# Output rows of two batches in nine 128-row blocks, and the folds of the modes in units 12 to 14

## The chip, the cores and the metric

The kernel runs on one core of one Trainium2 chip. The metric is the device time of one execution, in microseconds (us); the lower the better. Engines are named as in the profile: PE is TensorE's matmul, PEld its weight load, DVE is VectorE, ACT ScalarE, POOL GpSimd, SP SyncE.

## What is computed

A causal attention with decay over 8 batches, 8 heads, 576 positions and 64 elements a head, and then a layer that multiplies the lowest 64 Fourier modes of its input by complex 512 x 512 matrices:

```python
def _attn_ref(q, k, v, f):
    scores = scale * np.matmul(q, k.transpose(0, 1, 3, 2))
    cum = np.cumsum(np.log(np.clip(f, 0.0001, 1.0)), axis=-1)
    scores = np.where(causal, -1e9, scores + cum[:, :, :, None] - cum[:, :, None, :])
    ...
    return np.matmul(attn, v)

def _moe_ref(x, w_r, w_i, w_ch):            # x: 8 batches x 576 positions x 512
    X = np.fft.rfft(x, axis=1)              # 64 modes are kept: Xr, Xi
    Yr = np.einsum('bmd,mde->bme', Xr, w_r) - np.einsum('bmd,mde->bme', Xi, w_i)
    Yi = np.einsum('bmd,mde->bme', Xr, w_i) + np.einsum('bmd,mde->bme', Xi, w_r)
    ...
    y = np.fft.irfft(Y, n=S, axis=1)
    u = x + y
    return u + np.maximum(u @ w_ch, 0.0)
```

The two weight arrays are 64 MB each as given (64 x 512 x 512 x 4 bytes) and are read once. Inputs and output are f32; the kernel computes in bf16 with f32 sums.

## The kernel before

All instructions are issued in the order of the program text; no scheduler moves them. Each engine works through its own instructions in that order and waits on semaphores where it needs another's result.

**First stage: attention.** 32 pairs of heads, each with its loads, transposes, scores, exponentials and sums; x ends up in `x_all` (128 rows x 4 element blocks x 8 batches x 5 position blocks x 128). The 576 positions of a batch are five blocks: four of 128 and one of 64 (`SBLK`). Beside it run the Fourier sums of x (`XS`, `XP`) and the first weight tiles.

**The weights** are loaded by POOL, in tiles of 1 MB (`issue_w`, L140). Tile (u, dc) holds the four modes of unit u for the 128-row slice dc of both arrays (dc 0 and 1), or for a 256-row slice of one array (dc 2 and 3). The order is `wseq`: at the end (12, 1), (12, 2), (12, 3), (13, 1), ... (15, 3). The tiles lie in `wpool` (7 buffers); a load waits until the tile seven places ahead of it has been used. The very last tile, (15, 3), is loaded in four pieces of 256 KB, one for each mode.

**Second stage: the units** (loop at L717, u from 0 to 15). For each tile, `spec_mms` multiplies the Fourier columns by the weights, 8 matmuls on TensorE, into one PSUM tile `A`; at the end of a unit VectorE adds what the early tiles had given (`Yb`, L745), four matmuls turn it (`yps`, L748) and VectorE copies it to `YT` (modes of units 0 to 11) or `YL` (modes of units 12 to 15). The last unit is computed turned at once by `spec_cols` (L198, 32 matmuls a tile), its sum kept in `accT`. In units 2 to 10, `xw` computes x times w_ch for one batch each into `XW`. Batches 3 to 7 of `XW` lie in a buffer that the profile calls `yx`.

**The folds** (L670 to L714). From unit 12 on the modes of units 0 to 11 are complete, and the kernel adds their share of y to x and of y times w_ch to `XW`, in place, batch by batch: `fold_modes(b)` (8 matmuls, two copies on ScalarE) and `fold(b, ...)` (for each of five position blocks: two matmuls for `pu`, copied to `x_all` by ScalarE, and one for `pz`, added to `XW` by VectorE). Before the change two batches are folded in each of the units 12 to 15, at dc 1 and 2, ahead of the unit's matmuls for that tile; the last three position blocks of batch 7 come after `spec_cols` of tile (15, 2).

**Third stage: the output** (from L764). For a block of rows two PSUM tiles are made: U = x plus the modes of units 12 to 15, and Z = the same times w_ch. `bases` starts them with x and `XW` (a matmul by the identity, 128 or 64 rows in the contraction), `rest` adds the last 32 mode rows of the batch (contraction 32, from one of four 32-row groups of `BI4` and `yl`). Then ScalarE copies U to `u_sb` (L855), VectorE computes max(Z, 0) + U into `o_sb` (L856), and SP stores it (L861, L866). A block of before (`blocks`, `parts`) is one position block of two batches: two tiles of 128 rows, or, for the fifth position block, one tile in which each batch has 64 rows. There are 16 and 4 of these. `U`, `Z` and the sums of the last modes share two PSUM pools of four tiles each (`psU`, `psZ`).

`last_modes(h)` (L809) makes `yl[h]`, the last modes of four batches: 4 matmuls that turn `YL` (`pyl`), 8 that multiply it by w_ch (`pywl`), one copy on ScalarE and one on VectorE. It runs for h = 0 ahead of the first block, after the last tile of weights has been used (`AT2`, L837) and added into `YL` (L840), and for h = 1 ahead of block 7.

Of the kernel before, what the change touches and what calls it, by code (L numbers as in the profile page):

```python
# [10 lines left out]
F32 = mybir.dt.float32  # L11
BF16 = mybir.dt.bfloat16
I32 = mybir.dt.int32
ALU = mybir.AluOpType
# [3 lines left out]
def _strided(ap: bass.AP, free_dims, offset_elems: int = 0) -> bass.AP:  # L18
    new_ap = [list(ap.ap[0])] + [list(x) for x in free_dims]
    return bass.AP(tensor=ap.tensor, offset=ap.offset + offset_elems, ap=new_ap)  # L20
# [3 lines left out]
def kernel(  # L24
# [11 lines left out]
    nc = tc.nc  # L36
    B, H, S, Dh = q.shape
# [586 lines left out]
    with ExitStack() as bctx:  # L624
# [8 lines left out]
        with ExitStack() as mctx:  # L633
# [59 lines left out]
                nc.scalar.copy(yw_sb[:KF, :], pyw[:KF, :])  # L693
                return y_sb, yw_sb

            def fold(b, ys, sbs):

                y_sb, yw_sb = ys
                for sb in sbs:
                    Ms = SBLK[sb]  # L700
                    bi = BI[:KF, sb * 128 : sb * 128 + Ms]
                    pu = psX.tile([128, D], F32, tag="x", name="pu")
                    nc.tensor.matmul(
                        pu[:Ms, :], lhsT=ident_bf[:Ms, :Ms], rhs=x_all[:Ms, :, b, sb, :], start=True, stop=False
                    )
                    nc.tensor.matmul(pu[:Ms, :], lhsT=bi, rhs=y_sb[:KF, :], start=False, stop=True)  # L706
                    nc.scalar.copy(  # L707
                        x_all[:Ms, :, b, sb, :], pu[:Ms, :].rearrange("p (g c) -> p g c", g=NEB)
                    )
                    pz = psX.tile([128, D], F32, tag="x", name="pz")  # L710
                    nc.tensor.matmul(pz[:Ms, :], lhsT=bi, rhs=yw_sb[:KF, :], start=True, stop=True)
                    nc.vector.tensor_tensor(
                        XW[b][:Ms, sb, :], pz[:Ms, :], XW[b][:Ms, sb, :], ALU.add
                    )  # L714

            xw_plan = {2: 0, 3: 1, 5: 2, 6: 3, 7: 4, 8: 5, 9: 6, 10: 7}
            for u in range(NU):  # L717
# [4 lines left out]
                for dc in range(first, NEB - 1 if last else NEB):  # L722
                    if dc == NEB - 1 and u in xw_plan:
                        xw(xw_plan[u])
                    split = NSB
                    if u >= NF and dc < 3:
                        b = 2 * (u - NF) + dc - 1
                        split = 2 if b == B - 1 else NSB
                        ys = fold_modes(b)
                        fold(b, ys, range(split))  # L730
                    if last:
                        AT = psA.tile([128, NEB, 8, B], F32, tag="a", name="AT1")
                        spec_cols(AT, dc)
                        nc.vector.tensor_tensor(
                            accT[:], AT[:].rearrange("p e c b -> p e b c"), accT[:], ALU.add
                        )
                    else:
                        spec_mms(A, u, dc, dc == first, dc == NEB - 1)
                    issue_w()
                    if split < NSB:  # L740
                        fold(b, ys, range(split, NSB))
                if last:
                    break
                Yb = ybpool.tile([128, D], BF16, tag="yb", name="Yb")
# [19 lines left out]
        usb = bctx.enter_context(tc.tile_pool(name="usb", bufs=4))  # L764
        psU = bctx.enter_context(tc.tile_pool(name="psU", bufs=4, space=PSUM))
        psZ = bctx.enter_context(tc.tile_pool(name="psZ", bufs=4, space=PSUM))
        blocks = [(p, sb) for p in range(B // 2) for sb in range(NSB)]
        yl = {}

        def parts(n):  # L770

            p, sb = blocks[n]
            Ms = SBLK[sb]
            if sb < NSB - 1:
                return [(2 * p + k, k, slice(0, Ms), sb, Ms) for k in range(2)]
            return [(2 * p + k, 0, slice(Ms * k, Ms * k + Ms), sb, Ms) for k in range(2)]

        def bases(n):

            pts = parts(n)  # L780
            nt = 1 + pts[1][1]
            U = [psU.tile([128, D], F32, tag="u", name="U") for _ in range(nt)]
            Z = [psZ.tile([128, D], F32, tag="z", name="Z") for _ in range(nt)]
            for which, ps in enumerate((U, Z)):
                for b, k, rows, sb, Ms in pts:
                    nc.tensor.matmul(  # L786
                        ps[k][rows, :],
                        lhsT=ident_bf[:Ms, :Ms],
                        rhs=XW[b][:Ms, sb, :] if which else x_all[:Ms, :, b, sb, :],
                        start=True,  # L790
                        stop=False,
                    )
            return U, Z

        def rest(n, U, Z):

            for which, ps in enumerate((U, Z)):
                for b, k, rows, sb, Ms in parts(n):
                    r = (b + 2 * which) % 4
                    grp = slice(32 * r, 32 * r + 32)  # L800
                    nc.tensor.matmul(
                        ps[k][rows, :],
                        lhsT=BI4[grp, sb * 128 : sb * 128 + Ms],
                        rhs=yl[b // 4][which][grp, :],
                        start=False,
                        stop=True,
                    )

        def last_modes(h):  # L809

            py = psU.tile([128, D], F32, tag="u", name="pyl")
            for eb in range(NEB):
                nc.tensor.matmul(
                    py[:, eb * 128 : (eb + 1) * 128],
# [2 lines left out]
                    start=True,  # L817
                    stop=True,
                )
            pyw = psZ.tile([128, D], F32, tag="z", name="pywl")  # L820
            for eb in range(NEB):
                for n in range(2):
                    b = 4 * h + 2 * (1 - n)
# [4 lines left out]
                        start=(eb == 0),  # L828
                        stop=(eb == NEB - 1),
                    )  # L830
            yl[h] = [ylpool.tile([128, D], BF16, tag="yl", name="yl") for _ in range(2)]
            nc.scalar.copy(yl[h][0][:], py[:])
            nc.vector.tensor_copy(yl[h][1][:], pyw[:])

        first = bases(0)
        AT = psU.tile([128, NEB, 8, B], F32, tag="u", name="AT2")
        spec_cols(AT, NEB - 1)  # L837
        for h in range(2):
            bs = slice(4 * h, 4 * h + 4)
# [3 lines left out]
                accT[:, :, bs, :],  # L843
                ALU.add,
            )
        last_modes(0)
        for i, (p, sb) in enumerate(blocks):
            if i == 7:
                last_modes(1)
            U, Z = first if i == 0 else bases(i)  # L850
            rest(i, U, Z)
            o_sb = wpool.tile([128, 2, D], F32, tag="w8", name="o_sb")
            for n in range(len(U)):
                u_sb = usb.tile([128, D], F32, tag="usb", name="u_sb")
                nc.scalar.copy(u_sb[:], U[n][:])  # L855
                nc.vector.scalar_tensor_tensor(  # L856
                    o_sb[:, n, :], Z[n][:], 0.0, u_sb[:], ALU.max, ALU.add
                )
            s0 = sb * 128
            if len(U) == 2:  # L860
                nc.sync.dma_start(  # L861
                    out[2 * p : 2 * p + 2, s0 : s0 + 128, :].rearrange("b p e -> p b e"), o_sb[:]
                )
            else:
                for b, k, rows, _, Ms in parts(i):
                    nc.sync.dma_start(out[b, s0 : s0 + Ms, :], o_sb[rows, 0, :])  # L866


# [28 lines left out]
```

## Time and profile before

| | |
|---|---|
| time, median of 3 runs | 442.19 us (442.12 to 442.97) |
| the profiled execution: time | 442.61 us |
| the profiled execution: span of the core | 439.5 us |
| mean granted TensorE clock | 0.936 of full |
| PE busy | 346.6 us (79%) |
| DVE busy | 268.7 us (61%) |
| ACT busy | 233.3 us (53%) |
| DMA | 96.75 MB, mean 220 GB/s |

The span is the time from the first to the last instruction of the core; the time of a run has some 3 us around it. The busy shares are means over stages with different limits, so what a change in one stage does is read from that stage. All times of instructions below count from the start of the span. A matmul row such as "128*64 128x512" means 128 rows of contraction, 64 output rows (columns of the array) and a moving operand of 512 columns; the end of a matmul in the profile is modelled, so it is the distance from start to start that tells how long it holds the engine.

### The profile page before, as it was taken

The page shows a single profiled execution, that of the slowest core. Times are in us where ns is not written, and L with a number is a line of the kernel's source. Part 1 is how long each engine was busy: PE and PEld are TensorE (multiplying, and loading weights), DVE is VectorE, ACT ScalarE, POOL GpSimd, SP SyncE. Part 2 cuts the span into 40 slices and gives each one's busy share as a digit, 9 for nine tenths or more (in the row PEclk, how much of TensorE's full clock was granted, in tenths as well). Part 3 has the DMA queues.
Part 4 walks back from the last instruction along what each step waited for, and adds up shares of the span by engine and source line. Part 5 has one row for each costly group of instructions (what it writes and reads, how often), then busy time and mean ns, then how long its engine had stood idle before and what let it go on. Part 6 is the DMA issues. An engine that isn't in the chain of part 4 may idle for free.

```text
span 439.5 us, 10294 instructions
## 1 busy us (share of the span) xinstructions
PE 346.6 (79%) x4305; PEld 190.0 (43%) x4305; DVE 268.7 (61%) x641; ACT 233.3 (53%) x355; POOL 130.5 (30%) x201
## 2 busy tenths in 40 slices
PE   2678787888888989889793496697797688989993
PEld 1455555555555565555461232343333233334330
DVE  7588889777887778888871221223223255464884
ACT  6558767778777666566550022133222355454673
POOL 6544445434554444444213111112202221100000
PEclk9999999999999999999997589599979699799997
DMA  8999999999999999999999999999999999994698
GB/s 151 230 233 220 232 220 233 230 226 230 234 229 224 229 224 229 223 229 225 233 214 211 212 212 212 212 212 212 212 212 211 210 210 210 210 210 81 233 354 275
DMA packets 68221, 96.75 MB, mean 220 GB/s; under 512 B 3536, under 2 KB 45008, under 8 KB 68176
## 3 DMA queue, kind: packets, MB, share of 16 engines
q0 software_dynamic: 62960, 86.23, 105.5%
q1 hardware_dynamic: 5216, 9.88, 6.4%
q8 instruction: 33, 0.54, 0.4%
q14 instruction: 12, 0.10, 0.1%
HBM read 163.73 MB, written 9.44 MB: 394 GB/s over the span
## 4 chain that ended last, share of the span: by engine, by line
DMA 39%; PE 34%; DVE 19%; ACT 3%; issue 3%; POOL 1%; DVEq 0%; POOLq 0%; ACTq 0%
DMA w<-in_moe_w_i_dram 22%; DMA w<-in_moe_w_r_dram 15%; DVE vT L385 5%; DVE x_all L493 4%; DVE qkT L361 4%; PE pav L478 4%; PE A L194 4%; PE sps L433 3%; PE tv L383 3%; PE pd L522 3%; PE vp L394 2%; PE U L786 2%; PE Z L786 2%; DMA qk<-in_k_dram 2%; DVE vn L373 2%
## 5 line engine op out<-in xcount | busy, mean ns | idle before, releaser
L440 ACT ACTIVATE et<-sps 128x1024 bf16<-128x1024 f32 x96 | 96.0, 1050 | 12.5 <-PE sps L433 11.1
L478 PE MATMUL pav<-vs,et 128*128 128x65 bf16 (+1 forms) x896 | 51.3, 197 | 0.2 <-DVE vn L373 0.2
L745 DVE TENSOR_TENSOR Yb<-A,yx 128x512 bf16<-128x512 f32 x15 | 10.4, 692 | 65.2 <-PE A L194 65.2
L361 DVE COPY qkT<-tp 128x640 bf16<-128x640 bf16 x64 | 48.8, 763 | 1.4 <-PE tp L356 1.3
L478 PEld LDWEIGHTS <-et 128*128 128x128 bf16 (+1 forms) x896 | 36.5, 102 | 17.2 <-issue 13.3
L194 PE MATMUL A<-w,XP 128*16 128x512 bf16 (+1 forms) x240 | 23.0, 465 | 24.7 <-DMA w<-in_moe_w_i_dram 14.0
L661 PE MATMUL pxw<-wch,xT 128*128 128x512 bf16 (+1 forms) x160 | 40.9, 411 | 0.0
L433 PE MATMUL sps<-qkT 64*128 64x512 bf16 (+4 forms) x320 | 38.9, 306 | 1.1 <-DVE qkT L361 1.1
L493 DVE TENSOR_TENSOR x_all<-pav,rcp 128x384 bf16<-128x384 f32 (+2 forms) x96 | 36.2, 377 | 3.3
L356 PE MATMUL tp<-ident_bf,qk 128*64 128x128 bf16 x576 | 29.4, 232 | 8.6 <-DMA qk<-in_k_dram 8.6
L385 DVE COPY vT<-tv 128x576 bf16<-128x576 bf16 x32 | 24.2, 757 | 18.6 <-PE tv L383 18.6
L668 ACT CAST XW<-pxw 128x512 bf16<-128x512 f32 (+1 forms) x15 | 8.8, 585 | 47.7 <-PE pxw L661 47.7
L668 ACT CAST yx<-pxw 128x512 bf16<-128x512 f32 (+1 forms) x25 | 14.6, 585 | 34.5 <-PE pxw L661 34.5
L156 POOL DMA_DIRECT2D w<-in_moe_w_r_dram x27 | 20.5, 759 | 41.7 <-PE A L194 10.1
L165 POOL DMA_DIRECT2D w<-in_moe_w_r_dram x16 | 11.9, 741 | 69.8 <-PE A L194 44.7
L405 ACT COPY vs<-vp 128x576 bf16<-128x576 bf16 x32 | 20.5, 640 | 21.4 <-PE vp L401 21.4
L109 POOL DMA_DIRECT2D qk<-in_q_dram x32 | 19.6, 611 | 36.9 <-PE tp L356 9.0
L165 POOL DMA_DIRECT2D w<-in_moe_w_i_dram x19 | 13.2, 697 | 57.5 <-PE A L194 35.1
L707 ACT CAST x_all<-pu 128x512 bf16<-128x512 f32 (+1 forms) x40 | 23.4, 584 | 8.4 <-PE pu L706 7.5
L373 DVE TENSOR_TENSOR vn<-vt,wn 128x576 bf16<-128x576 f32 x32 | 23.8, 744 | 4.6 <-ACT wn L298 2.7
L492 DVE RECIPROCAL rcp<-pav 128x6 f32<-128x6 f32 (+2 forms) x96 | 16.2, 169 | 16.1 <-PE pav L478 16.0
L652 DVE COPY xT<-ptr 128x576 bf16<-128x576 bf16 x32 | 14.6, 458 | 18.1 <-PE ptr L647 17.4
(134 smaller groups left out, 669.3 us busy)
## 6 DMA issues: line engine op xcount, KB each, us to landing
w<-in_moe_w_r_dram POOLq DMA_DIRECT2D x16, 1024.0 KB, 29.7
w<-in_moe_w_i_dram POOLq DMA_DIRECT2D x15, 1024.0 KB, 31.6
w<-in_moe_w_r_dram POOLq DMA_DIRECT2D x27, 512.0 KB, 11.0
w<-in_moe_w_i_dram POOLq DMA_DIRECT2D x27, 512.0 KB, 12.6
vt<-in_v_dram POOLq DMA_DIRECT2D x31, 288.0 KB, 10.6
out_dram<-o_sb SPq DMA_DIRECT2D x16, 512.0 KB, 3.8
qk<-in_q_dram POOLq DMA_DIRECT2D x32, 144.0 KB, 10.7
qk<-in_k_dram POOLq DMA_DIRECT2D x32, 144.0 KB, 10.4
```

The source lines that it names most:

```text
L165: nc.gpsimd.dma_start(w8[:, j : j + step, :, :].rearrange("p m r e -> p m (r e)"), src[m : m + step, 256:512, :].rearrange("m (p r) e -> p ...
L194: nc.tensor.matmul(A[32 * j : 32 * j + M, :], lhsT=lhsT, rhs=rhs, start=st_, stop=sp_)
L356: nc.tensor.transpose(tp[64 * hp : 64 * hp + 64, r - r0, :, :].rearrange("p n c -> p (n c)"), qk[:, hp, r * 64 : r * 64 + 64], ident_bf[:, :],
L361: nc.vector.tensor_copy(st[i]["T"][:].rearrange("p n (c r) -> p n c r", r=9)[:, :, :, r0:r1], tp[:, 0 : r1 - r0, :, :].rearrange("p r n c ...
L373: nc.vector.tensor_tensor(vn[:], st[i]["vt"][:], _strided(wn[:, widx(i), :], [[1, 9], [0, Dh]]), ALU.mult)
L385: nc.vector.tensor_copy(st[i]["vT"][:].rearrange("p (c r) -> p c r", r=9), tv[:].rearrange("p r c -> p c r"))
L433: nc.tensor.matmul(ps[:, hp, c : c + n], lhsT=KT[sl, jb * 128 : jb * 128 + 128], rhs=QT[sl, i0 : i0 + n], start=True, stop=True,)
L440: nc.scalar.activation(st[i]["et"][:, T, :, :], ps[:], ACT.Exp, scale=scale)
L478: nc.tensor.matmul(pav[:Ms, sb % 3, hp, :], lhsT=eblk(i, hp, jb, sb), rhs=rhs, start=(jb == 0), stop=(jb == sb),)
L493: nc.vector.tensor_tensor(x_all[:ns, g, b, lo:hi, :].rearrange("p s (h d) -> p s h d", h=2), pav[:ns, lo % 3 : lo % 3 + n, :, 0:Dh], _stri ...
L661: nc.tensor.matmul(pxw[:Ms, :], lhsT=xT[:, eb, sb * 128 : sb * 128 + Ms], rhs=wch[:, eb, :], start=(eb == 0), stop=(eb == NEB - 1),)
L668: nc.scalar.copy(XW[b][:Ms, sb, :], pxw[:Ms, :])
```

## The change

- **Folds.** `fold` does all five position blocks at once, and three batches are folded in each of the units 12 and 13 (at dc 1, 2 and 3) and two in unit 14. None is left in unit 15.
- **Blocks of the output.** The 1152 rows of two neighbouring batches are taken together and cut in nine blocks of 128 (`cuts`): four in the first batch, one with 64 rows of each, four in the second batch, which start at position 64. The position blocks of `x_all` and `XW` are unchanged, so a block of the second batch has its bases from two matmuls of 64 rows: rows 64 to 127 of one position block go to output rows 0 to 63, rows 0 to 63 of the next to output rows 64 to 127. Its `rest` is one matmul for each of U and Z.
- **Steps.** There are 18 steps, two pairs of batches (P) times nine (n), each with two tiles: block n of the first two batches of P's four and block 8 - n of the other two. Every step has two full tiles, one ScalarE copy and one VectorE operation for each, and one store of 512 KB; the first and the last step store each tile by itself.
- **The first step.** All its bases for U and Z come ahead of the last tile of weights, as before. `last_modes` is taken apart: the copy of Z's modes is made in two halves on ScalarE and VectorE, U's `rest` comes ahead of it, and the sums for the other four batches (h = 1) are made in steps 0 and 1 instead of ahead of block 7.

```diff
                 nc.scalar.copy(yw_sb[:KF, :], pyw[:KF, :])
                 return y_sb, yw_sb
 
-            def fold(b, ys, sbs):
+            def fold(b, ys):
 
                 y_sb, yw_sb = ys
-                for sb in sbs:
+                for sb in range(NSB):
                     Ms = SBLK[sb]
                     bi = BI[:KF, sb * 128 : sb * 128 + Ms]
                     pu = psX.tile([128, D], F32, tag="x", name="pu")
@@ -722,12 +722,9 @@
                 for dc in range(first, NEB - 1 if last else NEB):
                     if dc == NEB - 1 and u in xw_plan:
                         xw(xw_plan[u])
-                    split = NSB
-                    if u >= NF and dc < 3:
-                        b = 2 * (u - NF) + dc - 1
-                        split = 2 if b == B - 1 else NSB
-                        ys = fold_modes(b)
-                        fold(b, ys, range(split))
+                    b = 3 * (u - NF) + dc - 1
+                    if 0 <= b < B:
+                        fold(b, fold_modes(b))
                     if last:
                         AT = psA.tile([128, NEB, 8, B], F32, tag="a", name="AT1")
                         spec_cols(AT, dc)
@@ -737,8 +734,6 @@
                     else:
                         spec_mms(A, u, dc, dc == first, dc == NEB - 1)
                     issue_w()
-                    if split < NSB:
-                        fold(b, ys, range(split, NSB))
                 if last:
                     break
                 Yb = ybpool.tile([128, D], BF16, tag="yb", name="Yb")
@@ -764,51 +759,53 @@
         usb = bctx.enter_context(tc.tile_pool(name="usb", bufs=4))
         psU = bctx.enter_context(tc.tile_pool(name="psU", bufs=4, space=PSUM))
         psZ = bctx.enter_context(tc.tile_pool(name="psZ", bufs=4, space=PSUM))
-        blocks = [(p, sb) for p in range(B // 2) for sb in range(NSB)]
+        rows_out = out.rearrange("b s e -> (b s) e")
+        steps = [(P, n) for P in range(2) for n in range(9)]
         yl = {}
 
-        def parts(n):
-
-            p, sb = blocks[n]
-            Ms = SBLK[sb]
-            if sb < NSB - 1:
-                return [(2 * p + k, k, slice(0, Ms), sb, Ms) for k in range(2)]
-            return [(2 * p + k, 0, slice(Ms * k, Ms * k + Ms), sb, Ms) for k in range(2)]
-
-        def bases(n):
-
-            pts = parts(n)
-            nt = 1 + pts[1][1]
-            U = [psU.tile([128, D], F32, tag="u", name="U") for _ in range(nt)]
-            Z = [psZ.tile([128, D], F32, tag="z", name="Z") for _ in range(nt)]
-            for which, ps in enumerate((U, Z)):
-                for b, k, rows, sb, Ms in pts:
+        def cuts(P, n, k):
+
+            n = 8 - n if k else n
+            b = 4 * P + 2 * k
+            if n < 4:
+                return [(b, 0, n, 0, 128)], [(b, 0, 128 * n, 128)]
+            if n == 4:
+                return [(b, 0, 4, 0, 64), (b + 1, 64, 0, 0, 64)], [(b, 0, 512, 64), (b + 1, 64, 0, 64)]
+            j = n - 5
+            return [(b + 1, 0, j, 64, 64), (b + 1, 64, j + 1, 0, 64)], [(b + 1, 0, 64 + 128 * j, 128)]
+
+        def bases(st_, ps, which):
+
+            for k in range(2):
+                for b, o, sc, lo, m in cuts(*st_, k)[0]:
                     nc.tensor.matmul(
-                        ps[k][rows, :],
-                        lhsT=ident_bf[:Ms, :Ms],
-                        rhs=XW[b][:Ms, sb, :] if which else x_all[:Ms, :, b, sb, :],
+                        ps[k][o : o + m, :],
+                        lhsT=ident_bf[lo : lo + m, lo : lo + m],
+                        rhs=XW[b][lo : lo + m, sc, :] if which else x_all[lo : lo + m, :, b, sc, :],
                         start=True,
                         stop=False,
                     )
-            return U, Z
-
-        def rest(n, U, Z):
-
-            for which, ps in enumerate((U, Z)):
-                for b, k, rows, sb, Ms in parts(n):
+
+        def rest(st_, ps, which):
+
+            for k in range(2):
+                for b, o, s0, m in cuts(*st_, k)[1]:
                     r = (b + 2 * which) % 4
                     grp = slice(32 * r, 32 * r + 32)
                     nc.tensor.matmul(
-                        ps[k][rows, :],
-                        lhsT=BI4[grp, sb * 128 : sb * 128 + Ms],
+                        ps[k][o : o + m, :],
+                        lhsT=BI4[grp, s0 : s0 + m],
                         rhs=yl[b // 4][which][grp, :],
                         start=False,
                         stop=True,
                     )
 
-        def last_modes(h):
-
-            py = psU.tile([128, D], F32, tag="u", name="pyl")
+        def two(pool, tag):
+            return [pool.tile([128, D], F32, tag=tag, name=tag.upper()) for _ in range(2)]
+
+        def modes_u(h, py):
+
+            yl[h] = [ylpool.tile([128, D], BF16, tag="yl", name="yl") for _ in range(2)]
             for eb in range(NEB):
                 nc.tensor.matmul(
                     py[:, eb * 128 : (eb + 1) * 128],
@@ -817,7 +814,9 @@
                     start=True,
                     stop=True,
                 )
-            pyw = psZ.tile([128, D], F32, tag="z", name="pywl")
+
+        def modes_z(h, pyw):
+
             for eb in range(NEB):
                 for n in range(2):
                     b = 4 * h + 2 * (1 - n)
@@ -828,12 +827,36 @@
                         start=(eb == 0),
                         stop=(eb == NEB - 1),
                     )
-            yl[h] = [ylpool.tile([128, D], BF16, tag="yl", name="yl") for _ in range(2)]
-            nc.scalar.copy(yl[h][0][:], py[:])
-            nc.vector.tensor_copy(yl[h][1][:], pyw[:])
-
-        first = bases(0)
+
+        def finish(U, Z, store):
+
+            o_sb = wpool.tile([128, 2, D], F32, tag="w8", name="o_sb")
+            for k in range(2):
+                u_sb = usb.tile([128, D], F32, tag="usb", name="u_sb")
+                nc.scalar.copy(u_sb[:], U[k][:])
+                nc.vector.scalar_tensor_tensor(
+                    o_sb[:, k, :], Z[k][:], 0.0, u_sb[:], ALU.max, ALU.add
+                )
+                store(o_sb, k)
+
+        def store_of(st_, single):
+
+            P, n = st_
+            R = [1152 * (2 * P) + 128 * n, 1152 * (2 * P + 1) + 128 * (8 - n)]
+
+            def store(o_sb, k):
+                if single:
+                    nc.sync.dma_start(rows_out[R[k] : R[k] + 128, :], o_sb[:, k, :])
+                elif k == 1:
+                    dst = rows_out[R[0] : R[0] + 128, :]
+                    nc.sync.dma_start(_strided(dst, [[(R[1] - R[0]) * D, 2], [1, D]]), o_sb[:])
+
+            return store
+
         AT = psU.tile([128, NEB, 8, B], F32, tag="u", name="AT2")
+        U, Z = two(psU, "u"), two(psZ, "z")
+        bases(steps[0], U, 0)
+        bases(steps[0], Z, 1)
         spec_cols(AT, NEB - 1)
         for h in range(2):
             bs = slice(4 * h, 4 * h + 4)
@@ -843,27 +866,30 @@
                 accT[:, :, bs, :],
                 ALU.add,
             )
-        last_modes(0)
-        for i, (p, sb) in enumerate(blocks):
-            if i == 7:
-                last_modes(1)
-            U, Z = first if i == 0 else bases(i)
-            rest(i, U, Z)
-            o_sb = wpool.tile([128, 2, D], F32, tag="w8", name="o_sb")
-            for n in range(len(U)):
-                u_sb = usb.tile([128, D], F32, tag="usb", name="u_sb")
-                nc.scalar.copy(u_sb[:], U[n][:])
-                nc.vector.scalar_tensor_tensor(
-                    o_sb[:, n, :], Z[n][:], 0.0, u_sb[:], ALU.max, ALU.add
-                )
-            s0 = sb * 128
-            if len(U) == 2:
-                nc.sync.dma_start(
-                    out[2 * p : 2 * p + 2, s0 : s0 + 128, :].rearrange("b p e -> p b e"), o_sb[:]
-                )
-            else:
-                for b, k, rows, _, Ms in parts(i):
-                    nc.sync.dma_start(out[b, s0 : s0 + Ms, :], o_sb[rows, 0, :])
+        py0 = psU.tile([128, D], F32, tag="u", name="pyl")
+        pyw0 = psZ.tile([128, D], F32, tag="z", name="pywl")
+        modes_u(0, py0)
+        nc.scalar.copy(yl[0][0][:], py0[:])
+        modes_z(0, pyw0)
+        rest(steps[0], U, 0)
+        nc.scalar.copy(yl[0][1][:, 0 : D // 2], pyw0[:, 0 : D // 2])
+        nc.vector.tensor_copy(yl[0][1][:, D // 2 : D], pyw0[:, D // 2 : D])
+        rest(steps[0], Z, 1)
+        pyw1 = psU.tile([128, D], F32, tag="u", name="pywl")
+        py1 = psZ.tile([128, D], F32, tag="z", name="pyl")
+        modes_u(1, py1)
+        finish(U, Z, store_of(steps[0], True))
+        nc.scalar.copy(yl[1][0][:], py1[:])
+        for i in range(1, len(steps)):
+            U, Z = two(psU, "u"), two(psZ, "z")
+            bases(steps[i], U, 0)
+            if i == 1:
+                modes_z(1, pyw1)
+                nc.vector.tensor_copy(yl[1][1][:], pyw1[:])
+            bases(steps[i], Z, 1)
+            rest(steps[i], U, 0)
+            rest(steps[i], Z, 1)
+            finish(U, Z, store_of(steps[i], i == len(steps) - 1))
 
 
 # ---- launch: one core; inputs and outputs as the reference has them ----
```

## The prediction

> **What bounds the kernel now.** I read the page's slices first (DMA at nine tenths for 36 of 40 slices, so almost all of the kernel is the stream of weights), then the DMA and PE views of the end of that stream, then the chain of waits behind it, because the diff touches only the time after 345 us.
>
> The end of the stream, in the timeline: the last issue on POOL, and TensorE's use of that tile (start, us).
>
> ```profile
> 383.74 0.53 POOL L165 DMA_DIRECT2D w<-in_moe_w_i_dram  x1 [4.92 <-DMA w<-in_moe_w_r_dram]
> ...
> 403.37 1.07 PE L211 MATMUL AT<-XP,w 128*128 128x16 bf16 x32
> ```
>
> The list of DMA issues, cut to that one (size, us to landing):
>
> ```profile
> w<-in_moe_w_i_dram POOLq DMA_DIRECT2D x1, 256.0 KB, 19.7
> ```
>
> Busy times by stretch (length; PE, PEld, DVE, ACT, POOL; clock, DMA share, GB/s):
>
> ```profile
> 403.00:404.00 1.00, 1.00 (x25) 0.76 (x25) 0.00 (x0) 0.00 (x0) 0.00 (x0) 1.00 0.03 8
> ```
>
> The last 256 KB of weights, issued at 383.74, land 19.7 later, at 403.44; the DMA rate is 8 GB/s in the microsecond around it, and 0 in the next. TensorE starts on this tile at 403.37. So two things end together there: the folds on TensorE and the stream. The chain of waits names TensorE only because it is the later by a hair.
>
> Behind that the chain is TensorE without a gap (start, us, what): one 64-row output block and one 128-row block.
>
> ```profile
> 424.99 0.33 PE U L786 x2
> 425.32 0.22 PE Z L786 x2
> 425.54 0.33 PE U L801 x2
> 425.87 0.01 PE Z L801 x2
> 425.88 0.54 PE U L786 x2
> 426.42 0.43 PE Z L786 x2
> 426.85 0.32 PE U L801 x2
> 427.17 0.01 PE Z L801 x2
> ```
>
> A 128-row block takes 1.30 (425.88 to 427.18), a 64-row block 0.89; 16 and 4 of them make 24.3 us; they and the second half's mode sums (L813 and L824, 1.3) fill 407.05 to 431.98. The first 512 KB store takes 2.8 from issue to landing; VectorE needs 0.65 for each output tile (nine in 5.88), so 1.31 per block, and ScalarE 1.07 for two: both just keep up.
>
> **The folds (units 12 to 14).** One fold is 5.13 on TensorE (359.86 to 364.99). After: unit 12 gets a third fold, so unit 13 starts at 359.86 + 5.13 = 364.99; its three folds and three weight tiles (0.55 each) and 0.93 for the way over Yb end at 382.96; unit 14 with two folds and three tiles at 395.8. All these tiles have landed by 388.4. Unit 15's first tile takes 0.9, to 396.7. Its second (issued 368.49, landing 30.0 later) comes at 398.5, the four chunks of its third between about 399.7 and 403.44. The later reads of tiles hold back issues on POOL: the tile of (15,1) is freed at 364 instead of 358.9, that of (15,3) at 376.4 instead of 371.2. The queue in front of them is 20 to 30 us deep (their times to landing), so the stream goes on and the landing at 403.44 stays; without that cover each us of lateness would cost one.
>
> What is gained: before, 32 matmuls followed 403.37 and the add to YL began at 404.48. After, 24 of them, at 0.028 each, are done as their chunks land; 8 remain, so YL starts at about 403.9: **-0.55**. The 15 us of work that leaves the stretch from 389.9 to 403.4 buys no more, since the stream ends it.
>
> **What the gap does to the clock.** TensorE now waits in most of 396.7 to 403.44 (0.9 for one tile, 1.2 for the first bases, 0.7 for three chunks). The trace shows what such a wait does. Windows of the clock's own grid (length, PE busy, granted clock, DMA share, GB/s):
>
> ```profile
> 304.50:307.91 3.41, 1.99 (x17) 1.00 1.12 210
> 338.63:342.05 3.42, 0.54 (x8) 0.99 1.18 207
> 342.05:345.46 3.41, 1.46 (x12) 0.50 1.19 208
> 345.46:348.87 3.41, 3.09 (x11) 0.51 1.15 212
> ...
> 369.35:372.77 3.42, 1.98 (x14) 0.99 1.19 208
> 372.77:376.18 3.41, 2.49 (x18) 0.50 1.19 211
> ```
>
> After a window with 1.98 or less of work the clock is halved for at least two windows; it comes back when these are filled. On this grid the next boundaries are 396.66, 400.07, 403.49, 406.90. The window to 400.07 would hold 0.9 + 0.6 of work, so the clock halves at 400.07 and returns at 406.90. In between lie, on the path: 8 matmuls (0.23 more at half clock), the transposing sum (0.43 for 0.24 in the folds at 345.78 and 390.02, so +0.25), and the second sum (0.98, all but its end at half clock: +0.9): **+1.4**. Bounds: the grid may lie otherwise. A boundary at 398.4 costs 0.8, one at 401.5 lets the clock fall only at about 404.9 and stay low to 411.7, which costs up to 3; none at all if TensorE comes to that gap late.
>
> **The head of the output.** The copy of the second sum (0.70 at 406.31, the bases of Z waiting for it) is cut in two halves on two engines: no such half is in the trace; between 0.35 (half) and 0.70, I take 0.42, nearest to half: **-0.3**. The 8+4 sums of the second half (1.3) move from block 7 to steps 0 and 1, where they partly cover the waits for buffers that step 0 holds: the U bases of step 1 wait for ScalarE's second copy, about 0.35. At full clock, with the gaps of before: YL 403.9, transposing sum 404.28, second sum 404.6, its copies 405.75, Z's modes 406.2, second half's first sum to 406.85, U bases to 407.5, second sum to 408.5, Z bases, and step 1's modes start at 409.15. Before, block 1's started at 408.35 with the 1.3 of sums still ahead.
>
> **The 18 steps.** Each step has one block of 128 rows in one batch (F) and, in its mirror, two pieces of 64 (a pair P), for U and for Z, then the modes R of K=32: F P F P R, or P F P F R. The 64-row blocks of before stood alone. What it costs to go from one shape to another, the timeline shows (start, us, matmul), in a fold's last block:
>
> ```profile
> 393.97 0.38 PE L711 MATMUL pz<-yw_sb,BI 96*128 96x512 bf16 x1
> 394.27 0.40 PE L703 MATMUL pu<-x_all,ident_bf 64*64 64x512 bf16 x1
> 394.60 0.40 PE L706 MATMUL pu<-y_sb,BI 96*64 96x512 bf16 x1
> 394.84 0.38 PE L711 MATMUL pz<-yw_sb,BI 96*64 96x512 bf16 x1
> 395.15 0.96 PE L211 MATMUL AT<-XS,w 128*128 128x16 bf16 x32
> ```
>
> From start to start: 0.30 from 128 columns to 64*64, 0.33 from there to 96*64, 0.24 within that shape, 0.31 out of it. Matmuls of one shape follow at 0.216 (393.75 to 393.97). So a change of shape adds 0.09 to 0.115, and a pair runs as one (two 64*64 in 0.24 at 418.75). A 128-row block has two changes, into and out of R: 5 x 0.216 + 0.22 = 1.30, as measured. A new step has five: 0.317 (R to F) + 0.307 + 0.330 + 0.307 + 0.306 = 1.567, or 0.315 + 0.330 + 0.307 + 0.330 + 0.312 = 1.594 in the other order. The step with n = 4 has pairs alone, but twice the modes, of which U's and Z's share row groups and go one after the other: 0.315 + 3 x 0.237 + 0.306 + 0.22 = 1.55. All 18: 8 x 1.567 + 8 x 1.594 + 2 x 1.55 = 28.4 against 24.3: **+4.1**. It is wholly on the path: VectorE (1.31), ScalarE (1.07) and a 512 KB store (385 GB/s at best in this stretch, 1.36) are all shorter. Bounds: 0 if the changes were hidden, +4.1; more only with the fourth rival.
>
> The Trainium skill, TensorEngine Tiling (Array Packing), section Key Properties, says that a change of tiling mode, unlike a change of tile, drains the array. It speaks against this mixing and gives no price; the rows above agree, at 0.09 to 0.115 each.
>
> **The end and the sum.** From the start of step 1's modes (409.15 at full clock) the other 16 steps, 25.25, lead to 434.4. The last modes to the end of the second tile: 2.33 (430.77 to 433.10 before). Its 256 KB store: before, a 512 KB one took 2.8 from issue to landing with queues empty and 128 KB took 4.2 behind a backlog; the slower steps leave none, I take 2.6. Landing to the end of the span: 1.2 (438.3 to 439.5). Full clock: 434.4 + 2.33 + 2.6 + 1.2 = 440.5; with the clock's 1.4: **441.9, against 439.5: +2.4**. In other words the last modes come 2.75 later at full clock (434.4 for 431.65), 1.7 of which the end gives back (6.1 for 7.85), since before a backlog of stores stood there (DMA full from 424 to 437), and the clock costs 1.4. The profiled execution took 442.61, 3.1 over its span and 0.42 over the median 442.19; +2.4 on the median is **444.6**.
>
> **Rivals.**
> 1. *The shape changes cost nothing here* (the pieces' weights are loaded ahead): steps of VectorE's 1.31 instead of 1.58, and soon DMA's 1.36. Modes of step 1 at 410.55, 16 x 1.33, then 2.33, 2.8 and 1.2: 438.2 or less; about 441, **faster**. It decides below some 1.42 per step. For it: two pieces in different quadrants could load early. Against: all five changes have a row, and none is free. 0.14.
> 2. *The clock stays up*, because TensorE reaches the gap late or the grid favours it: 440.5 span, 443.2. Against: every window under 1.98 in the rows dropped. 0.12.
> 3. *The clock falls late*, at a boundary after 404, and stays low into the steps: up to 1.6 more, 445.5 to 446.3. The Trainium skill, TensorE: Matmul & The Clock Gate, says that the window runs freely and does not restart with a kernel; no run here shows that. 0.20.
> 4. *The pair runs one after the other*: its two pieces come from different row halves and write one PSUM bank. 2 x 0.216 in 18 steps: +7.8, 452. The same skill's TensorEngine Tiling (Array Packing), Gotcha 1, says that row tiles may not use one bank at once. Against: the 32*64 modes of a 64-row block do just that and take 0.33, as those in separate banks do. 0.05.
>
> **How the numbers follow.** Forecast 0.49, rivals as given. The range 442.7 to 446.6 holds forecast, 2 and 3 (0.81); rival 1 lies below, rival 4 above. About 0.2% (0.9 us) is what a measurement can tell. Faster by more is most of rival 1: 0.13; within is its edge and that of rival 2: 0.06; slower 0.81.
>
> **What would show it.** PE's starts within a step: five gaps of 0.30 to 0.33 and steps near 1.58; no VectorE wait as the releaser. The last weights landing at 403.4 with TensorE waiting for them; a clock of 0.5 within 398 to 411. Steps of 1.3, or weights landing later than 404.5, would make the prediction wrong.

## The result, and the profile after

The changed kernel takes 447.53 us in the median of 5 runs (445.67 to 449.2) against 442.19 (441.04 to 443.06): a ratio of 1.0111, with an interval of 1.0071 to 1.015. By the ratio it is slower by 4.9 us, where +2.4 had been forecast: the side was right, the size too small by half, and 447.53 lies above the forecast's range (to 446.6).

The profiled execution has a span of 445.6 us (time 447.53, so 1.9 outside the span; the page before had 3.1 there, and the two spans differ by more than the times). Its chain of waits, from the last weights to the second step (start, us, what):

```profile
384.34 19.72 DMA w<-in_moe_w_i_dram
404.06 0.04 issue
404.10 0.42 PE AT L211 x8
404.52 0.02 issue
404.55 0.30 DVE YL L863
...
408.33 0.61 PE Z L795 x2
...
410.46 1.85 PE pywl L823 x8
412.31 1.10 PE Z L781 x3
413.42 0.53 PE U L795 x2
413.94 0.00 PE Z L795 x2
413.95 0.66 PE U L781 x3
414.60 0.66 PE Z L781 x3
415.26 0.32 PE U L795 x2
```

The chain before, at the same places:

```profile
404.48 0.30 DVE YL L840
...
406.31 0.70 DVE yl L833
407.01 0.04 issue
407.05 0.39 PE Z L801 x2
...
415.24 0.98 PE pywl L824 x8
```

After the change the chain starts with a transfer: TensorE waits for the last 256 KB, and only 8 matmuls and 0.49 us lie between the landing and the add to YL, where there were 1.04 (403.44 to 404.48). So the folds are out of the way, as the change says. But the 8 matmuls of the second half's sum take 1.85 at L823, where they took 0.98, and the modes of step 1 start only at 413.42. Behind that a step takes 1.64 (413.95 to 415.58), and the end follows 6.0 after the last modes, at 445.6.

The windows of the clock's grid show why the head is slow (length, PE busy, granted clock, DMA share, GB/s):

```profile
396.76:400.17 3.41, 1.62 (x54) 1.00 0.73 138
400.17:403.58 3.41, 2.89 (x31) 0.50 0.29 53
403.58:407.00 3.42, 2.68 (x26) 0.50 0.00 1
407.00:410.41 3.41, 2.97 (x15) 0.50 0.01 2
410.41:413.82 3.41, 3.41 (x17) 0.50 0.44 156
413.82:417.24 3.42, 3.42 (x26) 1.00 0.13 49
```

The clock falls behind the window with 1.62 of work, at 400.17, and is low for four windows, 13.65 us, until behind the first that is full. Before, the clock was 1.00 from 379.6 to 434.2.

### The profile page after: what moved, and what is told of

Read it like the earlier page. It is cut to its first block, busy times and chain, and to the rows that moved or that the text cites. A ratio compares the mean times of both kernels' runs of the same rounds, so it can differ in the third digit from the quotient of the medians.

```text
span 445.6 us, 10352 instructions
## 1 busy us (share of the span) xinstructions
PE 353.4 (79%) x4337; PEld 190.9 (43%) x4337; DVE 268.2 (60%) x641; ACT 233.8 (52%) x356; POOL 130.7 (29%) x201
## 4 chain that ended last, share of the span: by engine, by line
DMA 43%; PE 31%; DVE 18%; issue 3%; ACT 3%; POOL 1%; DVEq 0%; POOLq 0%; ACTq 0%
DMA w<-in_moe_w_i_dram 26%; DMA w<-in_moe_w_r_dram 15%; DVE vT L385 5%; DVE x_all L493 4%; DVE qkT L361 4%; PE pav L478 4%; PE A L194 3%; PE sps L433 3%; PE tv L383 3%; PE pd L522 3%; PE U L781 3%; PE Z L781 3%; PE vp L394 2%; DMA qk<-in_k_dram 2%; DVE vn L373 2%
## 5 line engine op out<-in xcount | busy, mean ns | idle before, releaser
L156 POOL DMA_DIRECT2D w<-in_moe_w_r_dram x27 | 20.5, 758 | 45.1 <-PE A L194 13.3
L405 ACT COPY vs<-vp 128x576 bf16<-128x576 bf16 x32 | 20.5, 640 | 21.4 <-PE vp L401 21.4
L837 DVE SCALAR_TENSOR_TENSOR o_sb<-Z,u_sb 128x512 f32<-128x512 f32 x36 | 23.2, 686 | 7.7 <-ACT u_sb L836 7.6
```

## The experiments

Every ratio is to the kernel before on the same chip. A difference of two ratios is given in us of 442. The changed kernel was not timed again beside the experiments, so a difference to it carries the intervals of both.

### e1_folds_back: the new output with the old folds

```diff
-                    b = 3 * (u - NF) + dc - 1
-                    if 0 <= b < B:
-                        fold(b, fold_modes(b))
+                    if u >= NF and dc < 3:
+                        b = 2 * (u - NF) + dc - 1
+                        ...
```

> The changed output (18 mixed steps, new first step), but the folds where they were before, in units 12 to 15. Theory (two costs: the empty stretch behind the folds halves TensorE's clock from 400.1 to 413.8, and a mixed step takes 1.64 instead of 1.30): TensorE has folds until 402, so the clock stays at 1.00 until the steps are done, the first weights-free work starts 0.5 later than in the changed kernel, the modes of step 1 start at about 409.8 instead of 413.36, steps stay at 1.64, span about 442, some 3.6 under the changed kernel and 2.5 over the kernel before. Rival A (the steps alone make the loss): no change, 445 to 446. Rival B (the clock alone makes it): span 439 to 440.

Measured: 1.0035 (1.0009 to 1.0062), 3.4 us under the changed kernel. In the profile the clock is 1.00 from 380.6 to 438.6, the steps take 1.64 and the span is 443.4 (some 442 expected); the add to YL, which starts the head, is at 405.24, and step 1's modes start 5.6 behind it, at 410.84 (409.8 expected). The forecast of 3.6 for the time holds; both rivals fall, since neither the steps alone (no change) nor the clock alone (equal to before) fits.

### e2_folds_only: the old output with the folds moved

```diff
-                        b = 2 * (u - NF) + dc - 1
+                    b = 3 * (u - NF) + dc - 1
+                    if 0 <= b < B:
+                        fold(b, fold_modes(b), range(NSB))
```

> The kernel before with nothing changed but the folds, moved to units 12 to 14. Theory: the clock falls at about 400 and is low through the head of the output and perhaps the first blocks; the last tile's sum is 0.5 earlier, the sums behind it and two or three blocks take twice their time: 2.5 to 3.5 over the kernel before, blocks at 1.30 behind that. Rival A (steps alone): 0 to 0.5 faster than before. Rival B (clock alone): 5 over before.

Measured: 1.0030 (1.0012 to 1.0047), 1.3 us slower than before: the same sign, less than forecast. The clock falls here too, at 401.5, but is back after 10.2 us, because the old head goes over to dense blocks sooner. Stores that stood in a queue at the end before may have room for a part of the delay, but the two profiles show little of that: from the landing of the last weights TensorE's last modes end 2.5 us later than before (30.3 for 27.8), as expected, and the span ends 2.2 later (38.3 for 36.1). Why the time shows 1.3 stays open; its interval reaches to 2.1. Blocks take 1.30 as ever. Both rivals fall: A said 0 to 0.5 faster, B 5 slower.

### e3_fill: work in the gap that nobody needs

```diff
+    def spin(ps, n):
+        for _ in range(n):
+            nc.tensor.matmul(ps[:], lhsT=ident_bf[:, :], rhs=wch[:, 0, :], start=True, stop=True)
...
+                        spin(psX.tile([128, D], F32, tag="x", name="pf"), 7 if dc == 1 else 2)
...
-        spec_cols(AT, NEB - 1)
+        spec_cols(AT, NEB - 1, lambda j: spin(pyw0, (0, 1, 4, 0)[j]))
```

> The changed kernel with 14 matmuls of 128x512 added whose results nobody reads: 7 behind the sum of tile (15,1), 2 behind (15,2), 1 and 4 behind the second and third piece of (15,3), all in time in which TensorE waits for weights. Theory: the windows of the clock's grid between 396.7 and 403.5 are filled, the clock stays at 1.00, and in spite of 3 us more work the span falls by 3 to 4 us, to about 442; the steps stay at 1.64. Rival (the wait for weights or the new head itself holds step 1 back, not the clock): no change or up to 0.5 slower.

Measured: 1.0013 (0.9994 to 1.0033), 4.3 us under the changed kernel, by adding 14 matmuls. The chain of this kernel over the same stretch as above:

```profile
405.70 0.38 ACT yl L882
406.08 0.02 issue
406.10 0.44 DVE yl L883
406.54 0.04 issue
406.58 0.39 PE Z L802 x2
406.97 0.33 PE pyl L817 x4
407.30 0.55 PE U L788 x3
407.85 0.98 PE pywl L830 x8
408.84 0.66 PE Z L788 x3
409.49 0.32 PE U L802 x2
```

The second sum is back to 0.98, and step 1's modes start 5.6 after the add to YL (403.87) instead of 8.9. The clock is 1.00 from 349.7 to 438.5. This is the clock's price in the changed kernel, shown: 4.3 us in the time, 3.3 of them in the head of these two profiles. The steps are still 1.64 (409.82 to 411.46).

### e4_two_changes_fewer: the same matmuls in another order

```diff
+        def both(st_, U, Z):
+            for k in range(2):
+                for ps, which in ((U, 0), (Z, 1)):
+                    for b, o, sc, lo, m in cuts(*st_, k)[0]:
...
-            bases(steps[i], U, 0)
             if i == 1:
...
-            bases(steps[i], Z, 1)
...
+            else:
+                both(steps[i], U, Z)
```

> The changed kernel with the bases of steps 2 to 17 in another order: both U and Z of the first tile, then both of the second, so that the shape of the matmul changes three times in a step instead of five. Same matmuls, same count. Theory (a change of shape costs 0.09 to 0.115): 1.64 becomes about 1.41 to 1.43, 16 steps save 3.4 to 3.7 us of the span; VectorE (1.31 a step) and the stores (1.36) are still shorter. Rival (the step is paced by VectorE, ScalarE or the buffers): unchanged, 1.64.

Measured: 1.0047 (1.0026 to 1.0068), 2.8 us under the changed kernel. A step in its chain of waits:

```profile
426.13 0.32 PE U L793
426.45 0.22 PE Z L793
426.66 0.33 PE U L793 x2
427.00 0.22 PE Z L793 x2
427.21 0.32 PE U L807 x2
427.53 0.01 PE Z L807 x2
```

1.41 a step (426.13 to 427.54) with the very matmuls that took 1.64: the second of two equal shapes takes 0.22, a change of shape 0.32 or 0.33. That is 0.11 for each of the two changes left out. The time gains less than 16 times 0.22 and less than the 3.4 to 3.7 expected: the stores (1.36 for 512 KB) then have little slack. DMA's share is over 0.93 in all but one of the 2 us stretches from 420 to 442, and from the last modes (437.23) to the end of the span (444.7) it is 7.5, where the changed kernel has 6.0.

### e5_fill_head: three matmuls in the head's short waits

The clock's fall had been forecast, its stay had not. This kernel leaves the gap as it is and fills only what TensorE waits behind it.

```diff
+        spec_cols(AT, NEB - 1, lambda j: spin(pyw0, (0, 0, 1, 1)[j]))
...
         rest(steps[0], U, 0)
+        spin(py0, 1)
```

> The changed kernel with three matmuls of 128x512 added whose results nobody reads, only in short waits of the head behind the fall of the clock: one between the last two pieces of the weights, one in the wait for YL, one in the wait for the copies of yl. The empty stretch before it stays, so the clock falls at about 400 as in the changed kernel. Theory (the clock comes back only behind a window of its grid that is filled; the head's own short waits of 0.35 to 0.45 keep two windows from it): the window from 403.6 is full, the clock is back after 6.8 us instead of 13.65, the span falls by 2.5 to 3.5 us. Rival (it comes back after a fixed time, or by something else than the fill): low for 13.65 as before, span unchanged or 0.5 longer.

Measured: 1.0083 (1.0052 to 1.0114), 1.2 us under the changed kernel in the time, though the intervals overlap; the mechanism shows in the profile:

```profile
396.76:400.17 3.41, 2.51 (x43) 0.98 0.61 115
400.17:403.58 3.41, 2.38 (x39) 0.50 0.15 26
403.58:407.00 3.42, 3.42 (x14) 0.52 0.01 2
407.00:410.41 3.41, 3.41 (x27) 1.00 0.42 149
```

The window from 403.58 is full now, and the clock is back behind it: 6.8 us low instead of 13.65. The weights landed 1.9 earlier against the grid in this execution, so the window holds another part of the head than in the changed kernel; without the added matmul of 0.54 it would have held some 2.9 (an estimate from its rows). From the add to YL (402.71) to the end of the span (441.5) it is 38.8 us, where the changed kernel has 41.1: 2.3 less, just under the 2.5 to 3.5 that were expected, and the time gains only half of that. A fixed time is ruled out: the clock is low for 6.8 here, 10.2 in e2 and 13.65 in the changed kernel.

### e6_fill_and_order, e7_folds_back_and_order: both costs away

These put the edits of e3 and e4 (e6) and of e1 and e4 (e7) together, with nothing added.

> e3_fill and e4_two_changes_fewer together: clock kept at 1.00 through the gap, three changes of shape in a step. Theory: step 1.42, so TensorE would be 3.5 us earlier than in e3_fill; but from there the stores (1.36 us per 512 KB at 376 KB per us) pace the end, and of 3.5 some 2.5 arrive: span about 439, 0.5 to 1.5 under the kernel before at the same landing of the weights. Rival (the shape changes and the clock are one and the same loss, or the end has another bound): no more than 1 us better than e3_fill.

> e1_folds_back and e4_two_changes_fewer together: folds where they were before, 18 steps with three changes of shape each. Theory: e1_folds_back less 16 times 0.22 on TensorE, less what the stores' backlog takes back: 2.5 to 3 us under e1_folds_back, between 0.5 faster than the kernel before and 1 slower. Rival: within 1 us of e1_folds_back.

Measured: 0.9992 (0.9973 to 1.0011) and 1.0013 (0.9994 to 1.0032). In e6 the clock is 1.00 from 349.4 to 434.7; in the profile of e7 it was 0.50 from 389.7 to 393.1, among the folds, and the add to YL came 2.4 behind the landing of the last weights, where it comes 1.4 behind it in e1. With the clock kept from there on and three changes of shape instead of five, the new output is as fast as the old, not faster; e6 gains 0.9 us on e3, e7 1.0 on e1, which is what the rival of each allowed, and under the 2.5 that the theory asked; against the kernel before, e7 lies where the theory had it, e6 just short of it. The stores take more of it than I reckoned: in e6 TensorE is done with its steps at 433, and DMA is full to 437. That they pace the end is read from this one profile; no run takes them away.

### e8_folds_and_fill: the folds' move by itself

```diff
+                        spin(psX.tile([128, D], F32, tag="x", name="pf"), 7 if dc == 1 else 2)
...
+        spec_cols(AT, NEB - 1, lambda j: spin(pyw0, (0, 1, 4, 0)[j]))
...
-        last_modes(0)
+        last_modes(0, pyw0)
```

That is e2 with the gap filled; the output is that of before.

> The output of before, the folds in units 12 to 14 (e2_folds_only), and the gap filled with the 14 matmuls nobody reads. Theory (moving the folds gains only that 24 of the last tile's 32 matmuls are done when its last piece lands, if the clock is kept): clock 1.00, 0.3 to 0.7 us faster than the kernel before. Rival A (the folds' move gains nothing even so): same as before. Rival B (it frees more than that, 15 us of work being out of the way): 2 or more faster.

Measured: 0.9969 (0.9951 to 0.9988), 1.4 us **faster** than before (0.5 to 2.2), the clock 1.00 from 348.3 to 433.7. So the move is worth something once the clock does not pay for it; the interval holds the upper part of the theory's 0.3 to 0.7, leaves out rival A, and B's 2 us stands at its edge. The profiles speak for the theory: from the landing of the last weights to the end of the span it is 35.5 us (402.8 to 438.3), where before it is 36.1, that is 0.5 less.

### e9, e10, e11: where the second half's sums stand

In e8 the new head was missing. e9 is e3 with the old blocks in its steps, and so has it:

```diff
-        steps = [(P, n) for P in range(2) for n in range(9)]
+        steps = [(p, sb) for p in range(B // 2) for sb in range(NSB)]
...
+            if sb < NSB - 1:
+                b = 2 * p + k
+                return [(b, 0, sb, 0, 128)], [(b, 0, 128 * sb, 128)]
```

> e8_folds_and_fill with the changed kernel's head: the blocks of before (16 of two 128-row tiles, 4 of 64 rows, no mixed shapes), folds in units 12 to 14, the gap filled with the 14 matmuls nobody reads, the copy of Z's modes in two halves, the second half's sums in steps 0 and 1, the first block's tiles stored one by one. Theory (the head itself was an improvement, hidden by clock and mixed shapes): Z's first modes 0.3 earlier than in e8_folds_and_fill, 0.2 to 0.8 us off the span, the stores then pacing all of the end; 0.4 to 0.5 percent faster than the kernel before. Rival (the waits that the moved sums meet in steps 0 and 1 give it back): equal to e8_folds_and_fill or slower.

Measured: 0.9992 (0.9975 to 1.0009): by the medians not better than e8 but 1.0 us worse, though the intervals overlap. The 0.3 expected of the head is not there: Z's first modes come 2.71 behind the add to YL, in e8 2.59. SP's issues in its timeline:

```profile
408.95 1.52 SPq L859 DMA_DIRECT2D out_dram<-o_sb  x2
412.72 3.06 SPq L861 DMA_DIRECT2D out_dram<-o_sb  x3
```

Between the first block's stores and the second's lie 3.8 us, and DMA stands nearly still from 412 to 414. e10 and e11 put the sums of the second half back ahead of block or step 7, e10 in e9 and e11 in e6:

```diff
+            if i == 7:
+                modes_u(1, py1)
+                modes_z(1, pyw1)
...
-            if i == 1:
-                modes_z(1, pyw1)
```

> e9_blocks_of_before_new_head with one thing undone: the sums of the second half stand ahead of block 7 again instead of in steps 0 and 1. Theory (moved into the head they put 1.4 us between the first block's stores and the second's, and the stores pace the end, so that time is never made up): the second block's store is issued 1.3 to 1.6 us after the first block's instead of 3.8, the span is 1 to 2 us under e9_blocks_of_before_new_head at the same landing, and 0.3 to 0.6 percent under the kernel before. Rival (e9 was slow for another reason, and the sums cost the same wherever they stand): equal to e9, 0.1 percent under before.

> e6_fill_and_order (18 steps with three changes of shape, gap filled) with the sums of the second half ahead of step 7 instead of in steps 0 and 1. Theory: as e10, the stores begin without a gap, 1 to 2 us under e6_fill_and_order, 0.2 to 0.5 percent under the kernel before. Rival: equal to e6_fill_and_order, that is the kernel before within 0.2 percent.

Measured: 0.9961 (0.9940 to 0.9983) and 0.9972 (0.9951 to 0.9994). The same lines of e10:

```profile
408.44 0.93 SPq L859 DMA_DIRECT2D out_dram<-o_sb  x2
410.90 3.06 SPq L861 DMA_DIRECT2D out_dram<-o_sb  x3
```

2.5 us instead of 3.8, more than the 1.3 to 1.6 expected. In the time the step is 1.4 us for e10 and 0.9 for e11, as expected in sign and rough size, but the intervals of each pair still overlap, those of e6 and e11 by half. e10, e8 and e11 beat both kernels, with intervals wholly under 1; among themselves they can't be told apart.

## Why the prediction was wrong in size

**The step that failed** is the clock's: "the clock halves at 400.07 and returns at 406.90 ... **+1.4**". It halved at 400.17 and came back at 413.82. I had taken from the windows before that it comes back after two windows "when these are filled", and then counted the head as filling them. The stretch up to step 1 fills none: at half clock it is still a chain in which TensorE waits for VectorE, the weights and ScalarE. In the first window it waits 0.52 for the sum of the tile before, in the second 0.35 for the last weights and 0.39 for YL, in the third 0.44 for the copies; that leaves 2.89, 2.68 and 2.97 us of work. Only the sums for the second half at L823 and the bases of step 1 fill one. So the head, from the add to YL to step 1's modes, took 8.9 instead of the 5.6 of e3 and e1, and the 8 matmuls ahead of it 0.42 instead of 0.24: some 3.4 us for the clock, where the sum had 1.4. e5 shows the cause, e3 and e1 the size.

The span (445.6) lies 3.7 over the forecast (441.9), and the modes of step 1 (413.42 instead of 410.55) account for 2.9 of that: 2.1 is the clock in the head, 0.4 a head that is longer even at full clock (5.6 for 5.25, the halved copy below), and 0.4 an add to YL that came later than forecast (404.55 for 404.13, which is 403.9 and the 0.23 of the clock), since the weights landed 0.6 later in this execution. The steps add 1.0, and the end takes some 0.15 less.

**The halved copy** is the second term that failed. The sum had -0.3 for it, with the two halves side by side. They run one after the other: in e3, at full clock, ScalarE's half ends at 406.08 and VectorE's runs from 406.10 to 406.54. In all ten kernels with this head the profile names ScalarE's half as what VectorE's waited for. From the add to YL to the first modes of Z it takes 2.71 in e3 (403.87 to 406.58), where it took 2.57 before (404.48 to 407.05) and 2.3 was forecast (403.9 to 406.2): 0.1 lost instead of 0.3 gained. The halves read one PSUM tile and write one tile; which of the two puts them in order, no run tells.

**The shapes** were right in mechanism and a little small: 1.64 instead of 1.58. A pair that stands alone between two other shapes takes 0.320 into it and 0.333 out of it, where I had 0.307 and, from two pairs in a row, 0.306. Sixteen steps took 26.2 instead of 25.25, 1.0 more. Rival 1 (changes that cost nothing) falls with every step in the trace, and e4, with two changes fewer, with its steps of 1.41. Rival 4 (the two pieces one after the other) falls too: a pair starts within 0.003 us and takes 0.33 in all.

**The folds** went as forecast: unit 13 starts its folds at 365.3 (364.99 forecast), the last tile of unit 15 waits for its landing, and the way from landing to YL shrinks by 0.55. **The end** took 6.0 from the last modes to the end of the span (6.13). Nothing shows that the later issues on POOL held up the stream: the last weights landed 0.6 later in this execution, but between 402.2 and 404.5 in the profiles of all thirteen kernels, both ends of that with the folds moved, and always 19.7 behind their issue.

**Rival 3** had the clock low into the steps, but for another reason, a fall that comes late. The fall came on time (400.2, 401.5 and 401.3 in the changed kernel, e2 and e4), also where the prediction had put it a window later: a boundary at 401.5 did not carry the clock to 404.9, and the windows ahead of it held 2.55 and 2.12, more than the 1.98 taken as the limit. Rival 2 (the clock stays up) falls with the four windows at 0.50. What was missing among the rivals is a clock that falls when forecast and does not return.

**Not in the prediction at all**: that the sums moved into the head hold up the second store. It was counted as cover for waits. In the changed kernel itself it can't be told from the clock's cost (its first block's stores are issued at 409.73, the next at 415.91); in e9 it shows.

The parts, in us: the folds alone cost 1.3 (e2), the new output alone 1.5 (e1), both together 4.9. Together the clock is low for 13.65 us, with the folds alone for 10.2; why the two together cost more than their sum was not tried. That the stores pay a part of a cost that comes alone is my reading; the profiles of e2 show little of it.

## What to carry to other kernels

Work moved off a stretch that waits for DMA anyway gains only what was behind the landing, and it can cost: here TensorE, left empty, went into the next stage at half clock. Before moving it, ask what is left to keep TensorE busy, and whether the stage behind is dense enough to bring the clock back; here a chain of small dependent steps was not. Count changes of matmul shape, not only matmuls, and group the equal shapes of several outputs: a change cost 0.11 here, about half of a 128x512 matmul (0.216). And where a copy is split over two engines, look in the trace whether the halves start together before a gain is booked for it.

## What the runs showed of the hardware

How full a window must be to bring the clock back, these traces do not say exactly. Windows of e2, the last before the fall and those behind it:

```profile
398.09:401.50 3.41, 2.55 (x52) 1.00 0.65 123
401.50:404.91 3.41, 1.86 (x24) 0.50 0.08 13
404.91:408.33 3.42, 3.10 (x14) 0.50 0.00 0
408.33:411.74 3.41, 3.41 (x12) 0.50 0.41 154
411.74:415.15 3.41, 3.41 (x25) 1.00 0.44 163
```

3.10 us of work did not bring it back here, 3.41 did. In the kernel before, 3.09 had been enough once (the row of 345.46 in the prediction), and once a full window was not:

```profile
249.89:253.30 3.41, 3.41 (x26) 0.50 1.12 211
253.30:256.71 3.41, 3.41 (x10) 0.51 1.12 212
```

Behind the second of these it was 1.00. So the busy time with its modelled ends does not give the threshold. Nor is the clock low for at least two windows each time, as the prediction read it: in e1 it was low for one, 3.41 us from 319.15, in the kernel before for six, 20.5 us from 236.2. And it fell behind a window of 2.55, where 1.99 had been borne at 304.50: much of those 2.55 are matmuls of 16 columns, whose modelled 0.19 us each overlap at distances of 0.03. What counts there may be the array's real work; no run tells it.

The Trainium skill, TensorE: Matmul & The Clock Gate, section Part 1: The HAM clock gate, says that the clock returns after at least one busy window of about 3.4 us and that the window does not restart with the kernel. The second agrees with falls at 400.2, 401.3 and 401.5 behind the same gap; the first leaves open how much counts as busy: three windows of the changed kernel with 78 to 87% of work did not do it, and the full one behind them did.
